# A set-attention and squared-ReLU kernel: the first batch planned anew, and second scores of the last batch made three groups at a time

## The chip, the cores and the metric

The kernel runs on one core of a Trainium2 chip. The metric is the device time of one execution in microseconds (us), the median of three runs. The engines are PE (matmul, with PEld for its weight loads), DVE, ACT, POOL and SP; SP issues all transfers here.

## The reference

`x` is (4, 12480, 128) in float32, `inducing` 32 points of 128. Two attentions follow each other, and an expert layer takes the result:

```python
def mab(q, kv):
    s = scale * (q @ kv.transpose(0, 2, 1))
    s = s - s.max(-1, keepdims=True)
    a = np.exp(s)
    a /= a.sum(-1, keepdims=True) + 1e-09
    return a @ kv
h = mab(I, x)            # the 32 points attend to all tokens of a batch
y = mab(x, h)            # every token attends to the 32 points
r = np.maximum(y @ w_in, 0.0)        # 128 -> 2048
out = (s * (r * r) + b) @ w_out      # 2048 -> 128
```

## The kernel before

**Tiles.** A batch has 12480 tokens: 26 blocks of 480 (`BLK`), 13 halves of two blocks, 7 groups of four blocks (`GR`); the last group, 6, has two. There are 104 blocks over four batches.

**The expert part** sets the pace. For a block and two of the 16 slices of 128 hidden units, `pair` (L917) makes two matmuls into an `h` buffer of PSUM (L928; three buffers, ring `h`), a relu `r` on ACT or DVE (L942, L944), a product with `h` on DVE (L965), a rounded square `g1` on ACT (L1010), and the rest `g2` on POOL or DVE (L987). `out_part` (L1024) multiplies these by `w_hi` and `w_lo`, the rounded and the remaining part of `w_out` times `s`: two matmuls of 480 columns in, six out (L1035). A block has eight pairs. The first eight pairs (`NATIVE`) take `w_out` unsplit in full float32, four passes each, and need no split halves. The weights of the first matmul, `wst`, are `w_in` times the attention's result, so that `y` itself is never made.

**The second attention** of a group is `attend` (L791): 8 score matmuls of 32 columns into the free one of two banks (`bank`), a transpose on DVE, maximum, subtraction, exponential on ACT, sum, reciprocal, product, transpose back, and a split into two halves `hl`, which SP spreads to tiles `a2t`. A block's output parts wait until the front work of the block before is done.

**The first attention** of the next batch runs beside it: `scores` (L681) per group, `top`, `values` (L717) per two groups, `sums`, `points`. A `visit` (L1073) lets PE make an attend's scores and up to two `side` units in a row, in one `h` buffer's halves; what it is made of says which block does what:

```python
ATTEND_AT = (2, 6, 10, 14, 18, 22)     # block of a batch at which group n + 1 is attended
SCORES_WITH, VALUES_WITH               # sides of these visits, per batch; VALUES_AT: alone
```

In the last batch there is no next one, so attends are alone.

**The opening** is batch 0's first attention, before any pair can start. `ORDER` (L66) is the order of SP's loads: `x` a group, `w_in` and `w_out` a chunk of 512 columns, `q` a group loaded already turned. For groups not in `TURNED`, PE turns each half with 8 transposes (`turn_x`, L444) and ACT copies it out. `p1_unit` makes a group's scores (L480), maximum on DVE (L484), exponentials (L493), their transposes (L500) and values (L511). The groups share four tiles, and turned copies share four others, so a load waits for the last use of its tile. Weights come as pairs of 32-bit words of float64 numbers and are made float32 by `narrow` (L324): three or four steps on DVE, two on ACT; `split_w_out` (L352) follows. After the last values come `h_sums`, `h_out` (hT, L620), `attend_first` (L837, block 0's attention weights by another way) and `w_first` (L624). Between these PE runs matmuls on zeros (`warm`, L1226).

**The order of work** comes from `Plan` (L95): every unit yields an engine, a planned duration and what it waits for, and the planner starts, per engine, the step with the least start time plus `WEIGHT` times urgency. Where a step may go to two engines, `LEAN` is added to their ends. The planned durations and urgencies are constants in the code; the result is a fixed order of instructions on each engine.

## Time and profile before

| what | us |
|---|---|
| median of three runs (lowest, highest) | 1551.55 (1551.47, 1551.56) |
| the profiled execution's own time | 1552.4 |
| its span, first to last instruction | 1550.6 |
| PE busy in the span | 1542.8 |
| DVE, ACT, POOL busy | 1469.9, 1482.0, 1471.1 |

Times in the profile are counted from the span's start. Busy time of PE is modelled for pipelined matmuls, so the distance from one matmul's start to the next tells more than the busy share. A mean granted clock of 1.00 is TensorE's higher level.

### The profile page before, as it was taken

The numbers are of one execution on the slowest core, as the hardware profiler recorded it, in microseconds if no ns is written. First come the engines' busy times: TensorE is split into PE (matmuls) and PEld (weight loads), VectorE is DVE, ScalarE is ACT, GpSimd is POOL, SyncE is SP. The second block draws the span as 40 slices with busy tenths as digits, with TensorE's granted clock in tenths as the row PEclk, the third lists the DMA queues.
The fourth block names the chain that finished last, engine by engine and source line by source line (L and its number), as shares of the span: only waits on it lengthen the run. The fifth ranks groups of instructions, "written<-read, shape, count | busy, mean of one in ns | idle before, by whom it ended". The sixth has DMA issues, their size and how long they took to land.

```text
span 1550.6 us, 24505 instructions
## 1 busy us (share of the span) xinstructions
PE 1542.8 (99%) x8135; PEld 1294.9 (84%) x8135; DVE 1469.9 (95%) x1648; ACT 1482.0 (96%) x1750; POOL 1471.1 (95%) x665
## 2 busy tenths in 40 slices
PE   9999999999999999999999999999999999999999
PEld 6688888888888888888888888888888888888887
DVE  5999999999999999999999999999999999999998
ACT  7899999999999999999999999999999999999998
POOL 0299999999999999999999999999999999999998
PEclk9999999999999999999999999999999999999999
DMA  8212321332233123123232321321313112112100
GB/s 300 64 56 80 122 72 71 114 130 96 68 111 115 39 103 115 39 103 115 71 85 80 118 76 66 115 80 65 112 60 96 32 52 71 40 44 71 57 22 32
DMA packets 53482, 130.12 MB, mean 84 GB/s; under 512 B 11262, under 2 KB 37758, under 8 KB 53358
## 3 DMA queue, kind: packets, MB, share of 16 engines
q1 hardware_dynamic: 53358, 128.56, 25.2%
q8 instruction: 66, 1.08, 0.3%
q14 instruction: 58, 0.48, 0.1%
HBM read 74.50 MB, written 25.56 MB: 65 GB/s over the span
## 4 chain that ended last, share of the span: by engine, by line
PE 96%; DMA 2%; DVE 1%; POOL 0%; issue 0%; ACT 0%; SPq 0%; ACTq 0%; DVEq 0%; POOLq 0%
PE x L1035 68%; PE h L928 23%; PE x L799 2%; PE h L742 1%; PE h L701 1%; DMA g<-in_w_in_dram 1%; DMA xn<-in_xQ_dram 1%; DMA s_sb<-in_s_rep_dram 0%; DVE g L965 0%; POOL g L987 0%; PE h L651 0%; ACT xn L214 0%; PE x L742 0%; PE x L511 0%; SPq L420 0%
## 5 line engine op out<-in xcount | busy, mean ns | idle before, releaser
L987 POOL TENSOR_TENSOR g<-g,g 128x960 fp32r<-128x960 f32 x657 | 1469.8, 2296 | 73.6 <-DVE g L965 67.8
L1035 PE MATMUL x<-g,w_hi 128*128 128x480 f32 x3296 | 1063.6, 375 | 0.0
L1010 ACT ACTIVATE g<-r 128x960 fp32r<-128x960 f32 (+1 forms) x805 | 796.2, 1029 | 16.5 <-DVE r L944 2.4
L965 DVE SCALAR_TENSOR_TENSOR g<-h,r 128x960 f32<-128x960 f32 x657 | 739.4, 1146 | 22.4 <-ACT r L942 14.2
L1035 PEld LDWEIGHTS x<-g,w_hi 128*128 128x128 f32 x3296 | 614.8, 187 | 91.8 <-POOL g L987 3.3
L942 ACT ACTIVATE r<-h 128x960 f32<-128x960 f32 x660 | 622.8, 969 | 27.3 <-PE h L928 26.3
L1035 PE MATMUL x<-g,w_lo 128*128 128x480 f32 x1648 | 617.3, 375 | 0.0
L928 PE MATMUL h<-a2t,wst 128*128 128x480 f32 x1664 | 484.7, 378 | 0.7 <-DVE g L965 0.7
L928 PEld LDWEIGHTS h<-a2t,wst 128*128 128x128 f32 x1664 | 306.6, 187 | 65.4 <-DVE x L805 7.3
L1035 PEld LDWEIGHTS x<-g,w_lo 128*128 128x128 f32 x1648 | 308.9, 187 | 42.8
L944 DVE TENSOR_SCALAR r<-h 128x960 f32<-128x960 f32 x172 | 197.7, 1150 | 9.5 <-PE h L928 7.1
L987 DVE TENSOR_TENSOR g<-h,g 128x960 fp32r<-128x960 f32 x167 | 192.6, 1154 | 12.7 <-ACT g L1010 1.3
L965 DVE SCALAR_TENSOR_TENSOR h<-h,r 128x960 f32<-128x960 f32 x167 | 193.1, 1157 | 6.4 <-ACT r L942 5.7
L1044 ACT ACTIVATE ob<-x,bias 128x480 f32<-128x480 f32 x103 | 68.0, 660 | 4.1 <-PE x L1035 3.9
L799 PE MATMUL x<-xt,hT 128*32 128x480 f32 x208 | 28.3, 578 | 0.0
L805 DVE STREAM_TRANSPOSE x<-x 128x480 f32<-128x480 f32 (+1 forms) x28 | 19.3, 688 | 2.2 <-PE x L799 2.1
L742 PEld LDWEIGHTS h<-xn,eT 128*32 128x32 f32 (+1 forms) x570 | 17.0, 109 | 5.0 <-issue 4.8
L823 DVE STREAM_TRANSPOSE x<-x 128x480 f32<-128x480 f32 (+1 forms) x28 | 19.5, 696 | 0.9
L742 PE MATMUL h<-xn,eT 128*32 128x128 f32 (+1 forms) x570 | 19.6, 273 | 0.0
L821 DVE TENSOR_TENSOR x<-x,l 128x480 f32<-128x480 f32 (+1 forms) x28 | 18.5, 661 | 0.7
L701 PE MATMUL h<-xt,ind_sb 128*32 128x480 f32 x156 | 19.1, 566 | 0.0
L810 DVE TENSOR_TENSOR x<-x,mx 128x480 f32<-128x480 f32 (+1 forms) x28 | 18.4, 656 | 0.1
(147 smaller groups left out, 375.4 us busy)
## 6 DMA issues: line engine op xcount, KB each, us to landing
xt<-in_xT_dram SPq DMA_DIRECT2D x41, 960.0 KB, 5.5
out_dram<-ob SPq DMA_DIRECT2D x104, 240.0 KB, 2.0
a2t<-hl SPq DMA_DIRECT2D x412, 60.0 KB, 2.0
xn<-in_xN_dram SPq DMA_DIRECT2D x18, 512.0 KB, 6.1
xn<-in_xN_dram SPq DMA_DIRECT2D x18, 448.0 KB, 6.7
r<-in_xH_dram SPq DMA_DIRECT2D x7, 480.0 KB, 8.2
xt<-in_xT_dram SPq DMA_DIRECT2D x7, 480.0 KB, 5.4
wst<-hl SPq DMA_DIRECT2D x48, 64.0 KB, 2.0
```

The costliest lines, as they stand in the source:

```text
L701: nc.tensor.matmul(ps[M * q:M * (q + 1), 0:BLK], ind_sb, xt[:, q], start=True, stop=True)
L742: nc.tensor.matmul(ps[M * c:M * (c + 1), 0:P], eT[0:rows, n], xn_tiles[b, g, half][0][0:rows, n - half * TH], start=m < P // M, stop=m + P ...
L799: nc.tensor.matmul(ps[M * q:M * (q + 1), 0:BLK], hT[:, 0:M], xt[:, q], start=True, stop=True)
L823: nc.vector.transpose(out=s, in_=s)
L928: nc.tensor.matmul(h[:, u, 0:BLK], wst[:, c * P:(c + 1) * P], A, start=True, stop=True)
L942: nc.scalar.activation(out=r, in_=hv, func=AF.Relu)
L944: nc.vector.tensor_scalar(out=r, in0=hv, scalar1=0.0, scalar2=None, op0=ALU.max)
L965: nc.vector.scalar_tensor_tensor(out=g, in0=hv, scalar=0.0, in1=r, op0=ALU.max, op1=ALU.mult)
L987: eng.tensor_tensor(out=g2, in0=g, in1=hi.bitcast(F32), op=ALU.subtract)
L1010: nc.scalar.activation(out=q["g1_t"][:, sl, :], in_=q["r_t"][:, sl, :], func=AF.Square)
L1035: nc.tensor.matmul(o, w, g, start=first and n == 0, stop=left == 0 and n == len(ops) - 1)
L1044: nc.scalar.activation(out=ob, in_=o, func=AF.Identity, bias=bias, scale=1.0 if scaled else s_sb)
```

## The change

**Opening.** `ORDER`, the homes of `x` (five tiles in place of four, `X_HOME`), and the planned durations are new; 54 single units get urgencies of their own (`URGENT`), and the planner adds 0.14 us when PE changes between tiled (32 columns) and whole matmuls. Group 6 is loaded turned as group 5 was; the turned loads have tiles of their own and wait for nothing. `x` 0's first half is loaded and turned in two parts. `s` and `b` are loaded last. `w_out`'s raw chunks get four tiles of their own, in which the split halves `w_hi` and `w_lo` are put later. In `narrow`, an ACT step may go to POOL; for three chunks (`POOLED`) a DVE step is made by ACT and POOL; the last product may go to POOL. The memset for the warming matmuls goes from POOL to DVE.

**Batch 0.** The scores of batch 1's groups 6, 4 and 5 (`GAP`) are made in the opening, once batch 0's values are done; their `x` is loaded there, and `attend(0, 0)` waits for two of them. The visits of batch 0 then have the sides that those of batches 1 and 2 have; values of groups 2 and 3 are no longer alone.

**Batch 3.** `LAST_WITH`: the scores of groups 2 and 3 are made in the visit of group 1, those of 5 and 6 in that of group 4. `turned_scores` transposes them into the SBUF tile `s`; `attend` of these groups then has no matmul and no first transpose, and its maximum and subtraction read that tile.

All other weights of the planner (`LEAN`, `R_LEAN`, `SLIP`, `OUT` and so on) have new values too.

```diff
--- before.py
+++ after.py
...
-LEAN = {'ACT': -0.5309, 'DVE': 0.6608}
-R_LEAN = {'DVE': -0.2301, 'ACT': -0.2128}
+LEAN = {'ACT': -1.8612, 'DVE': -0.9887}
+R_LEAN = {'DVE': -0.234, 'ACT': -0.174}
...
-TURNED = (5,)
-ORDER = (
-    ("x", 0), ("x", 1), ("w_out", 0), ("x", 2), ("w_out", 1), ("x", 3), ("w_in", 0), ("x", 4), ("w_in", 1),
-    ("w_in", 2), ("x", 5), ("x", 6), ("w_out", 2), ("q", 5), ("w_in", 3), ("w_out", 3),
-)
-WARM = 6
+TURNED = (5, 6)
+X_HOME = (4, 1, 3, 0, 3, 2, 1)
+GAP = (6, 4, 5)
+ORDER = (('x', 0), ('w_in', 1), ('x', 1), ('x', 2), ('w_out', 2), ('w_out', 1), ('w_in', 0), ('w_out', 3), ('x', 3), ('x', 4), ('x', 5), ('x', 6), ('n', 6), ('q', 5), ('w_in', 2), ('q', 6), ('w_in', 3), ('n', 4), ('n', 5), ('w_out', 0), ('s', 0))
+SWITCH = 0.14
+POOLED = (('w_in', 2), ('w_out', 0), ('w_out', 2))
+GAP_U = 107.5895
+WARM = 7
+URGENT = {
+    ('x', 3): -234.92,
+    ('w_in', 1): 384.17,
+    ('w', 1): 32.13,
+    ('n', 4): -165.82,
...
-SCORES_WITH = (((6,), (0, 1), (2, 3), (4, 5), (), ()), ((0, 1), (2, 3), (4, 5), (), (), ()), ((0, 1), (2, 3), (4, 5), (), (), ()))
+LAST_WITH = ((2, 3), (), (), (5, 6), (), ())
+SCORES_WITH = (((), (0, 1), (2, 3), (), (), ()), ((0, 1), (2, 3), (4, 5), (), (), ()), ((0, 1), (2, 3), (4, 5), (), (), ()))
-TOP_AT = (17, 11, 11)
-VALUES_WITH = (((), (), (), (), (0,), (2, 3)), ((), (), (), (0,), (1,), (2, 3)), ((), (), (), (0,), (1,), (2, 3)))
-VALUES_AT = (((1, 20),), (), ())
+TOP_AT = (11, 11, 11)
+VALUES_WITH = (((), (), (), (0,), (1,), (2, 3)), ((), (), (), (0,), (1,), (2, 3)), ((), (), (), (0,), (1,), (2, 3)))
+VALUES_AT = ((), (), ())
...
+                turn = SWITCH if u[9] is not None and u[9] != self.tiled else 0.0
+                able.setdefault(eng, []).append((at + turn + WEIGHT * urgency, at, engs[eng] + turn, u))
...
+    warm_sb = ew.tile([P, 512], F32R, name="g2", bufs=8)
+    nc.vector.memset(warm_sb.bitcast(F32), 0.0)
...
-    w_hi = const.tile([P, NF, P], F32R, name="w_hi")
-    w_lo = const.tile([P, NF, P], F32R, name="w_lo")
...
     def load_weight(gate, name, c):
-        turn, free = ring("g1", 4)
-        yield "SP", 0.45, free, *gate
...
-        raw = ew.tile([P, WC, 2], I32, name="g1", bufs=4)
+        if name == "w_in":
+            turn, free = ring("g1", 4)
+            yield "SP", 0.45, free, *gate
+            raw, used = ew.tile([P, WC, 2], I32, name="g1", bufs=4), ("g1", turn)
+        else:
+            yield "SP", 0.45, *gate
+            raw, used = w2_pool.tile([P, WC, 2], I32, name="w2"), ("raw used", c)
...
-        yield "ACT", 0.48
-        nc.scalar.activation(out=dst, in_=m, func=AF.Copy, scale=2.0**-20, bias=1.0)
+        yield dict(ACT=0.525, Pool=0.68), {"ACT": M_LEAN}, 0.0
+        if plan.eng == "ACT":
+            nc.scalar.activation(out=dst, in_=m, func=AF.Copy, scale=2.0**-20, bias=1.0)
+        else:
+            nc.gpsimd.tensor_scalar(out=dst, in0=m, scalar1=2.0**-20, scalar2=1.0, op0=ALU.mult, op1=ALU.add)
+        if name in POOLED:
+            yield "ACT", 0.525
+            nc.scalar.activation(out=m.bitcast(F32), in_=lo, func=AF.Copy, scale=2.0**-52)
+            yield "Pool", 1.37
+            nc.gpsimd.tensor_tensor(out=dst, in0=m.bitcast(F32), in1=dst, op=ALU.add)
+        else:
+            yield "DVE", 0.6, "both"
+            nc.vector.scalar_tensor_tensor(out=dst, in0=lo, scalar=2.0**-52, in1=dst, op0=ALU.mult, op1=ALU.add)
...
+        plan.set(used)
+        yield dict(DVE=0.6, Pool=1.37), 0.0, "both"
+        either().tensor_tensor(out=dst, in0=dst, in1=e.bitcast(F32), op=ALU.mult)
...
+    def split_weights(f, part):
...
+        at = w_order.index(f * P // WC)
+        return w2[at // 2][part][:, at % 2 * WC // P + f % (WC // P), :]
...
-        yield "ACT", 0.54, ("w_out", c)
-        nc.scalar.activation(out=w_hi[:, sl, :], in_=raw[:, sl, :], func=AF.Copy, scale=s_sb)
+        half = w_order.index(c) // 2
+        mine = w_order[2 * half:2 * half + 2]
+        yield "ACT", 0.615, "s", ("w_out", c), *[("raw used", n) for n in mine], ("w2", half - 1)
+        if half not in w2:
+            w2[half] = [w2_pool.tile([P, 2 * WC // P, P], F32R, name="w2") for _ in range(2)]
+        nc.scalar.activation(out=w_hi, in_=raw[:, sl, :], func=AF.Copy, scale=s_sb)
...
-            home["x", g] = g if g < 4 else 1 + (g - 4) % 3
+            home["x", g] = X_HOME[g]
...
+        for n, j in enumerate(turns):
+            home["xn", j] = xn[n % 4][0:T].rearrange("p n c -> p (n c)")
+        for n in range(SB):
+            home["xn", TURNED[0] * GR // SB + n] = turned_0[0:T, n * TH * P:(n + 1) * TH * P]
+        for g in TURNED[1:2]:
+            for n in range(SB):
+                t = p2.tile([P, 2, WC], F32, name="hl")
+                home["xn", g * GR // SB + n] = t[0:T].rearrange("p a t -> p (a t)")
...
-            yield "SP", 0.45, ("v done", j - 4)
-            nc.sync.dma_start(out=home["q"][j % 4], in_=xQ[j])
+            yield "SP", 0.45
+            nc.sync.dma_start(out=home["xn", j], in_=xQ[j])
...
-        yield "PE", 0.99, *waits, ("x half", j), ("v done", j - 4)
+        n = turns.index(j)
+        if j:
+            yield "PE", 0.88, "whole", *waits, ("x half", j), *([("v done", turns[n - 4])] if n > 3 else [])
+        else:
+            yield "PE", 0.44, "whole", *waits, ("x part", 0, 0)
...
+            if a and not j:
+                yield "PE", 0.44, "whole", ("x half", j)
...
-                "s": p1.tile([P, NG, BLK], F32, name="s"),
+                "s": st[0]["room"].rearrange("p (g t) -> p g t", g=NG) if b == 1 and GAP
+                else p1.tile([P, NG, BLK], F32, name="s"),
...
+    def turned_scores(b, g, ps, *waits):
+
+        rows = M * blocks_in(g)
+        yield "PE", 1.14, ("hT", b), ("x", b, g, 2), *waits
+        ps = ps()
+        scores_2(b, g, ps)
+        yield "DVE", 0.58
+        nc.vector.transpose(out=st[b]["s"][0:rows, g], in_=ps[0:rows, 0:BLK])
+        plan.set(("turned", b, g))
+
+    def attend(b, g, ps, *waits):
+        nb = blocks_in(g)
+        rows = M * nb
+        ahead = b == B - 1 and any(g in gs for gs in LAST_WITH)
+        if ahead:
+            yield "DVE", 0.57, ("turned", b, g), *waits
+            ps = ps()
+            s = ps[0:rows, 0:BLK]
+            v = s.rearrange("p (n i) -> p n i", i=M)
+            t = st[b]["s"][0:rows, g].rearrange("p (n i) -> p n i", i=M)
+        else:
+            yield "PE", 1.14, ("hT", b), ("x", b, g, 2), *waits
+            ps = ps()
+            scores_2(b, g, ps)
+            s = ps[0:rows, 0:BLK]
+            t = v = s.rearrange("p (n i) -> p n i", i=M)
...
-        yield "DVE", 0.58
-        nc.vector.transpose(out=s, in_=s)
-        yield "DVE", 0.57
-        mx = sm.tile([P, TB], F32, name="mx2")[0:rows]
-        nc.vector.reduce_max(out=mx, in_=v, axis=AX.X)
+        mx = ps[0:rows, BLK + TB:BLK + 2 * TB] if ahead else sm.tile([P, TB], F32, name="mx2")[0:rows]
+        nc.vector.reduce_max(out=mx, in_=t, axis=AX.X)
...
-        nc.vector.tensor_tensor(out=v, in0=v, in1=mx.unsqueeze(2).broadcast_to([rows, TB, M]), op=ALU.subtract)
+        nc.vector.tensor_tensor(out=v, in0=t, in1=mx.unsqueeze(2).broadcast_to([rows, TB, M]), op=ALU.subtract)
...
-                    yield (*want, ("ob", blk_g - 1) if blk_g else "first") if first else want
+                    start = [("ob", blk_g - 1)] if blk_g else ["first", *[("scores", 1, g) for g in GAP[0::2]]]
+                    yield (*want, *start) if first else want
...
-            side = []
+            side = [(turned_scores, b, g) for g in LAST_WITH[n]] if b == B - 1 else []
...
-                if n == 1:
-                    nc.sync.dma_start(out=s_sb, in_=s_rep)
-                    nc.sync.dma_start(out=b_sb, in_=b_rep)
-                plan.spawn(p1_work(n), FIRST + 0.1 * n)
+                plan.spawn(p1_work(n), FIRST + 0.1 * n + urgent("x", n))
                 for h in range(0 if n in TURNED else -(-blocks_in(n) // SB)):
-                    plan.spawn(turn_work(n, h), FIRST + 0.1 * n)
+                    plan.spawn(turn_work(n, h), FIRST + 0.1 * n + urgent("turn", n, h))
             elif what == "q":
                 yield from load_turned(n)
+            elif what == "s":
+                yield "SP", 0.9
+                nc.sync.dma_start(out=s_sb, in_=s_rep)
+                nc.sync.dma_start(out=b_sb, in_=b_rep)
+                plan.events["s"] = landing(1.0)
+            elif what == "n":
+                yield from load_xt((), 1, n, 1)
+                i = GAP.index(n)
+                plan.spawn(
+                    scores(1, n, (lambda: bank[1], lambda: hs[0][:, 0])[i % 2],
+                           ("p1", 0, NG - 1), *([("scores", 1, GAP[i - 2])] if i > 1 else [])),
+                    FIRST + GAP_U + i + urgent("n", n),
+                )
...
-    nc.gpsimd.memset(warm_sb.bitcast(F32), 0.0)
...
+        plan.set("warm done")
+
+    def h_free():
+        yield "SP", 0.0, "warm done", *[("scores", 1, g) for g in GAP[1::2]]
         plan.set(("h", 0))
...
-        plan.spawn(attend_first(lambda: bank[0]), FIRST)
+        plan.spawn(attend_first(lambda: bank[0]), FIRST + urgent("a"))
+        plan.spawn(h_free(), 0.0)
```

## Rows read from the trace of the kernel before

**Rows 1.** The page: busy time by engine, and shares of the last chain.
```profile
PE 1542.8 (99%) x8135; PEld 1294.9 (84%) x8135; DVE 1469.9 (95%) x1648; ACT 1482.0 (96%) x1750; POOL 1471.1 (95%) x665
...
PE 96%; DMA 2%; DVE 1%; POOL 0%; issue 0%; ACT 0%; SPq 0%; ACTq 0%; DVEq 0%; POOLq 0%
```

**Rows 2.** Windows, batches 0, 3: busy PE, PEld, DVE, ACT, POOL; clock, DMA, GB/s.
```profile
200.00:250.00 50.00, 50.00 (x239) 43.01 (x232) 48.24 (x52) 49.21 (x56) 50.00 (x23) 1.00 0.27 94
1350.00:1400.00 50.00, 50.00 (x238) 42.62 (x237) 49.05 (x51) 49.27 (x56) 50.00 (x24) 1.00 0.16 51
```

**Rows 3.** Timeline of PE in the opening: start, us, what, idle before.
```profile
4.40 1.93 PE L453 MATMUL h<-ident,xt 128*120 128x128 f32 x8
...
18.80 1.01 PE L480 MATMUL x<-r,ind_sb 128*32 128x480 f32 x8
...
20.77 1.08 PE L511 MATMUL x<-xn,eT 120*32 120x128 f32 x32
...
28.61 0.65 PE L500 MATMUL h<-ident,s 128*120 128x128 f32 x4
...
32.08 1.04 PE L453 MATMUL h<-ident,r 128*120 128x128 f32 x8
...
35.21 1.74 PE L511 MATMUL x<-xn,eT 120*32 120x128 f32 x44 [1.07 <-DMA xn<-in_xQ_dram]
...
46.36 1.06 PE L928 MATMUL h<-a2t,wst 128*128 128x480 f32 x4
```

**Rows 4.** Windows of the opening, as in rows 2.
```profile
0.00:10.00 10.00, 8.42 (x46) 5.55 (x46) 1.77 (x10) 3.91 (x6) 1.23 (x8) 1.00 0.70 221
10.00:28.00 18.00, 17.77 (x232) 11.63 (x232) 13.07 (x29) 16.39 (x33) 0.00 (x0) 1.00 1.01 406
35.00:45.00 10.00, 9.29 (x90) 6.60 (x91) 8.01 (x23) 5.61 (x12) 0.00 (x0) 1.00 0.10 41
```

**Rows 5.** Timeline of PE: a lone attend (batch 3), a visit (batch 0).
```profile
1214.65 0.59 PE L928 MATMUL h<-a2t,wst 128*128 128x480 f32 x2
1215.17 1.01 PE L799 MATMUL x<-xt,hT 128*32 128x480 f32 x8
1216.12 0.70 PE L1035 MATMUL x<-g,w_hi 128*128 128x480 f32 x2
1216.65 0.60 PE L928 MATMUL h<-a2t,wst 128*128 128x480 f32 x2
...
197.99 1.01 PE L799 MATMUL x<-xt,hT 128*32 128x480 f32 x8
200.54 0.70 PE L928 MATMUL h<-a2t,wst 128*128 128x480 f32 x2
```

**Rows 6.** Groups by shape: count, busy us, mean ns, idle before.
```profile
L987 POOL TENSOR_TENSOR g<-g,g 128x960 fp32r<-128x960 f32 x657 | 1469.8, 2296 | 73.6 <-DVE g L965 67.8 <-ACT g L1010 2.8 <-DVE x L821 1.2
...
L214 ACT COPY xn<-h 120x1024 f32<-120x1024 f32 x11 | 11.3, 1029 | 6.9 <-PE h L453 6.9
...
L810 DVE TENSOR_TENSOR x<-x,mx 128x480 f32<-128x480 f32 x24 | 15.8, 657 | 0.1
...
L348 DVE TENSOR_TENSOR w_in_sb<-w_in_sb,g 128x512 f32<-128x512 f32 x4 | 2.7, 682 | 0.0
...
L965 DVE SCALAR_TENSOR_TENSOR g<-h,r 128x960 f32<-128x960 f32 x657 | 739.4, 1146 | 22.4 <-ACT r L942 14.2
```

**Rows 7.** Chain that ended last, in the opening: start, us, what.
```profile
27.29 7.88 DMA xn<-in_xQ_dram
...
42.65 0.70 DVE wst L637
```

**Rows 8.** DMA issues: size of one, us to landing.
```profile
xt<-in_xH_dram SPq DMA_DIRECT2D x6, 480.0 KB, 6.4
...
g<-in_w_in_dram SPq DMA_DIRECT2D x4, 512.0 KB, 8.6
```

**Rows 9.** The same windows for the warming matmuls (L1231) alone.
```profile
38.00:46.40 8.40, 4.62 (x14) 2.47 (x14) 1.00 0.00 1
```

More of the change, by code (lines that the diff above doesn't have):

```diff
@@ L71 @@
 RUN = 512
+M_LEAN = 2.2035
 A_OFF = 19
@@ L121, in _step @@
             more = sum(w for w in waits if isinstance(w, float))
-            waits = [w for w in waits if not isinstance(w, float) and w != "both"]
-            self.units.append([unit, urgency + more, (ready, src), engs, waits, urgency, lean, None, both])
+            kind = True if "tiled" in waits else False if "whole" in waits else None
+            waits = [w for w in waits if not isinstance(w, float) and w not in ("both", "tiled", "whole")]
+            self.units.append([unit, urgency + more, (ready, src), engs, waits, urgency, lean, None, both, kind])
     def extend(self, us):
@@ L345, in narrow @@
         )
[L346 to L348 removed]
+        plan.set(used)
+        yield dict(DVE=0.6, Pool=1.37), 0.0, "both"
+        either().tensor_tensor(out=dst, in0=dst, in1=e.bitcast(F32), op=ALU.mult)
         plan.set(("g", e_turn))
         plan.set(name)
+    w2 = {}
+    w_order = [c for name, c in ORDER if name == "w_out"]
+    plan.events["w2", -1] = 0.0
+    def split_weights(f, part):
+        at = w_order.index(f * P // WC)
+        return w2[at // 2][part][:, at % 2 * WC // P + f % (WC // P), :]
     def split_w_out(c):
@@ L683, in scores @@
         rows = M * nb
-        if b not in st:
+        if b not in begun:
+            begun.add(b)
+            yield "DVE", 0.15, *waits
             d = st[b] = {
@@ L1034, in out_part @@
         for n, (w, g) in enumerate(ops):
-            nc.tensor.matmul(o, w, g, start=first and n == 0, stop=left == 0 and n == len(ops) - 1)
+            nc.tensor.matmul(o, w(), g, start=first and n == 0, stop=left == 0 and n == len(ops) - 1)
         used()
@@ L1051, in out_part @@
         plan.set(("ob", blk_g))
+    turned_0 = wst_pool.tile([P, F], F32, name="wst")
+    turns = [j for j in range(NSB) if j * SB // GR not in TURNED]
     w_out_raw = wst_pool.tile([P, NF, P], F32, name="wst")
@@ L1169, in tile_attn_relu2 @@
             for f, *args in (args[0], *args[1]) if f is visit else ((f, *args),):
-                if f in (scores, attend):
+                if f in (scores, turned_scores) or f is attend and not any(args[1] in gs for gs in LAST_WITH if args[0] == B - 1):
                     fetch(first + n - AHEAD, load_xt, *args, 1 if f is scores else 2)
```

243 lines of the change are left out of this document (152 added, 91 removed).

## The prediction

> **What bounds the kernel now.** I read three views in this order. First the page's busy shares and its chain: PE is busy 99% of the span and carries 96% of the chain that ended last, while DVE, ACT and POOL are each at 95 to 96% [rows 1]. A busy PE need not be PE at its peak, so I checked the spacing. The 50 us windows of batch 0 and of batch 3 both show PE at 50.00 [rows 2], and in the second 238 instructions, 8 of them the score matmuls of one attend. The other 230 are matmuls of 480 columns, which the planner spaces by 0.2134 us: 49.1 us, and the attend's 0.95 [rows 5] makes it 50. There is no slack on PE behind the opening. There, time falls only if PE gets less to do, and a plan with other weights can only lose.
>
> Second, the opening, where that does not hold: the first pair's matmul starts at 46.36 us, on a path of loads, ACT and DVE [rows 3]. Third, its windows: 221 GB/s of DMA in the first 10 us, then about 400 while loads are queued [rows 4]. The last output part and its store, which end the kernel, are not touched.
>
> **Term 1, PE work taken out behind the opening.** A lone attend costs PE more than its 8 score matmuls. Between the end of one pair of L928 (1214.65 + 0.427 = 1215.08) and the point from which the next matmuls are spaced normally (1216.65 − 0.427 = 1216.22) lie 1.14 us; from its first matmul to the next work it is 0.95 (1215.17 to 1216.12). A visit of an attend with two other groups takes 2.55 on that second count (197.99 to 200.54) [rows 5]. So two sides add 1.60, 0.80 each, and joining a visit instead of coming alone saves 1.14 − 0.80 = 0.34.
> - Scores of batch 1 for groups 6, 4 and 5 leave the visits of batch 0 for the opening: 3 × 0.80 = 2.40 us. Group 6 has half the blocks, but its matmuls run side by side, so I count it in full.
> - Values of groups 2 and 3, alone at block 20 before, join a visit: 0.34.
> - In the last batch groups 2, 3, 5 and 6 are scored inside two visits: 4 × 0.34 = 1.36.
>
> Sum 4.1 us, all on the path, since PE is the path. Against it: the four moved groups hold a half of an h buffer until DVE has transposed them into SBUF. The first batches do the same with two sides, and PE stays at 50.00 there [rows 2], so I count nothing; without that cover PE would lose a DVE operation of this size per moved group, 4 × 0.66 [rows 6] = 2.6 us at most. DVE's own work is unchanged in number: the transpose moves to the visit, and maximum and subtraction read SBUF instead of PSUM. The trace has no such form; the subtraction in PSUM [rows 6] is the nearest and stands for it, a tenth less or more. DVE has 2% left in batch 3 [rows 2], and saving 1.4 us of 370 asks 0.4% of it.
>
> **Term 2, the opening.** Up to the last value matmuls (35.21 + 1.74 = 36.95) PE works 32.6 us from 4.40 on, and waits 1.07 us for the turned copy of group 5 [rows 3]. SP issued that load only when an earlier buffer was free, and the path hangs on the transfer for 7.88 us [rows 7]. The change gives turned loads homes of their own, so that wait goes, and loads group 6 turned as well, so 8 transposes (1.04 us [rows 3]) and one ACT copy (1.03 us [rows 6]) go. PE alone would be done 2.1 us earlier, at 34.8.
>
> Is the DMA in time? Up to q5 there are 10.5 MB in the new order, up to q6 11.5 (a half of x 0.49, a weight chunk 0.52 [rows 8]). With 2.2 MB moved by 10 us and 0.41 MB per us from then on [rows 4], q5 is in at 10 + 8.3/0.41 = 30.2 and q6 at 32.7. The last x has five weights ahead of it, as before, and comes at 26.6. Late next is x3: three weights more stand ahead of it, 6.55 MB, in at 20.6, where its scores run at 18.80 now. PE then has left two full groups, each 2 × 1.04 of transposes, 1.01 of scores, 0.65 and 1.08 for exponentials and values [rows 3], 4.8 us; 2.7 for group 5, which has no transposes, and 1.9 for the smaller group 6: 14.2 us, and 34.8 again. So the gain up to here is 2.1. On SP's queue n6 waits for x3 and n4 for x6, with n5, w_out 0 and s behind; the DMA has a backlog until about 34 us, which covers these waits.
>
> From there to the first pair is a chain of 9.4 us through hT and attend_first [rows 3]. Two weight subtractions on DVE stand inside it; the first, 0.70 us at 42.65 [rows 7], delays it in whole, the second I count with 0.3. The new urgencies put the chain ahead of them: 1.0 us less. Term 2 is 3.1; I take 3.0.
>
> Against it: the three early scores put 2.4 us on PE, hidden by the 4.6 us of warming matmuls [rows 9], and 3 × 0.66 us on DVE [rows 6], which idles 2.0 us of the 10 from 35 to 45 [rows 4]; cost 0 to 2.0, taken as 0 because weight work leaves DVE for POOL. And w_out chunk 0 lands at about 40, last but for s. Its seven steps of narrowing, 0.4 to 0.7 us each after the row of L348 [rows 6], take five or six us with hand-overs: 46 to 50. Native pairs 0 and 1 need it, and pair 3 takes the g buffer after it. Until then PE has six pairs' first matmuls, the attend and pair 2's output, 2.6 + 1.1 + 1.6 = 5.3 us from 43.3. Cost 0 to 2, taken as 0: it is nearer to being covered. Better packing than I assume could bring the DMA's limit (33.1) instead of PE's, 1.7 more.
>
> Edits with no price of their own: the warm-up memset goes from POOL to DVE, both idle until x0 is in at 4.40; s and b are loaded last, for splits that wait for chunk 0 anyway; the split halves live where raw chunks were, read out by 50 and needed by pair 8 after eight native pairs.
>
> **Sum.** 4.1 + 3.0 = 7.1 us off the profiled execution's 1552.4 (span 1550.6): 1545.3. The median of the runs shown, 1551.55, is 0.85 below that execution, so 1544.5. A difference under 0.2%, 3.1 us, is about what this measurement cannot tell from none.
>
> **Rivals.**
> - **The opening gives nothing.** POOL waits 67.8 us now, nearly all before its first such operation [rows 6], and does nothing in the opening's windows [rows 4]; the change gives it additions of three weight chunks and offers it products of all. On 512 columns I estimate 2.30 × 512/960 = 1.2 us each, from the only POOL operation of that kind in the trace [rows 6]. If DVE is held back while one runs, six to eight of them take 7 to 10 us of DVE, far more than it has free, and 3 or more come to lie on the way to the first pair. For it: the 0.68 us of L348 was taken with POOL idle. Against: POOL is busy all the time later and DVE still does L965 in 1.15 [rows 6], about what its other operations on 960 columns take. Time 1551.55 − 4.1 = 1547.5; with 1.5 us lost, 1549. The Trainium skill (SBUF — State Buffer, the engine side) has the rule: a DVE operation with two SBUF inputs and a GpSimd operation take a shared port pair in turn, the later one blocked for the whole instruction. L965 reads h from PSUM and L348 has two SBUF inputs, so by that rule the price would be paid; no row before shows it. Chance 0.24.
> - **The opening gives more**, down to the DMA's limit and a quicker chain behind it: 4.1 + 6.4 off, 1541. Chance 0.16.
> - **DVE or ACT becomes the bound, and it is slower.** All the planner's weights move, the leans that split copies and squares between ACT and DVE among them. With DVE and ACT at 98% in batch 3 [rows 2], a wrong choice leaves PE short for a moment. Place: every block. Price: 103 blocks × 0.1 us = 10.3; with 7.1 gained, 1554.7. It decides from 0.07 us per block. For it, engines near 98%; against, a PE without gaps under the old weights. Chance 0.07.
> - **The change does not do what it says**: merged visits stall the pairs by what they save, and early scores meet their waits; 2.7 and at most 1 remain, 1548. Chance 0.05.
>
> **How the numbers follow.** Forecast 0.48: 1544.5, its own range 1542 to 1547.3. The range runs from 1540.5 (the larger opening gain) to 1549 (none, and 1.5 given back) and leaves out the slower case and the tails. Faster by over 3.1 us (under 1548.4): forecast, larger gain and two thirds of the first rival, 0.80. Within: 0.13. Slower: 0.07.
>
> **What would show it.** Right: the first L928 at about 43.3 instead of 46.36; the last value matmuls done by 35; two runs of L799 for three groups in batch 3, and PE at 50.00 in every window behind the opening. Wrong: waits of PE in those windows; the successor of L348 at over 0.7 us beside POOL; a granted clock under 1.00 in the opening; a first pair later than 45.

## The result and the profile after

The changed kernel takes 1567.36 us (median of four runs, 1567.02 to 1569.32) beside 1551.55 for the kernel before: ratio 1.0103 [1.009, 1.0116], 15.8 us slower, where 7 us less were forecast. The profiled execution is the longest of the four, 1569.3 (span 1567.5). Its page, and from the page of before the two groups that the prediction did not show:

```profile
PE 1551.4 (99%) x8123; PEld 1303.7 (83%) x8123; DVE 1480.5 (94%) x1656; ACT 1470.2 (94%) x1724; POOL 1475.9 (94%) x675
...
L1188 PE MATMUL x<-g,w 128*128 128x480 f32 x4944 | 1190.9, 377 | 0.9 <-DVE hl L983 0.5
```

```profile
L1035 PE MATMUL x<-g,w_hi 128*128 128x480 f32 x3296 | 1063.6, 375 | 0.0
L1035 PE MATMUL x<-g,w_lo 128*128 128x480 f32 x1648 | 617.3, 375 | 0.0
```

PE is busy 8.6 us longer than before [rows 1], though it has less to do, and one of its 4944 output matmuls takes 2 ns more, 377 for 375. Such a duration is longer than the distance between two matmuls, since they overlap, so I took the distance from each start to the next from the trace (pairs nearer than 240 ns, behind 100 us): 213.4 ns before, 215.6 after. 4944 x 2.2 ns is 10.9 us, spread over the whole kernel. It is not waiting: behind 60 us PE's waits come to 1.3 us after and 0.7 before (what PE waited for: us in total, times, longest):

```profile
PE x L1188 <- DVE hl L983: 0.5, 1, 0.5
PE x L1188 <- POOL g L1140: 0.4, 1, 0.4
PE h L1081 <- DVE g L1118: 0.4, 1, 0.4
```

```profile
PE h L928 <- DVE g L965: 0.7, 2, 0.4
```

Windows (columns as in [rows 2]) show PE full in batch 3 as before. Their counts of instructions do not compare: all 235 are whole matmuls here, while 8 of the 238 before are the scores of a lone attend. The other three rows are the opening's:

```profile
30.00:35.00 5.00, 4.06 (x39) 2.70 (x37) 3.62 (x9) 4.92 (x11) 0.00 (x0) 1.00 1.01 226
35.00:40.00 5.00, 2.18 (x64) 1.64 (x56) 0.53 (x3) 0.00 (x1) 0.00 (x0) 1.00 1.05 241
40.00:45.00 5.00, 3.48 (x33) 3.02 (x34) 2.87 (x9) 2.94 (x8) 2.50 (x3) 0.66 0.98 382
...
1350.00:1400.00 50.00, 50.00 (x235) 43.60 (x233) 47.44 (x46) 48.34 (x57) 49.17 (x23) 1.00 0.26 90
```

From 30 to 40 us the DMA engines are busy all the time and move 226 to 241 GB/s, not about 400 [rows 4]; DVE (0.53 us) and ACT all but stand still from 35 to 40, PE works 2.2 us of 5, and behind that pause its granted clock falls to 0.66 on the mean of five microseconds. The chain of waits names the transfer, the turned copy of group 6, and what it delays:

```profile
29.76 12.01 DMA hl<-in_xQ_dram
...
55.71 1.74 DVE w L460
57.45 0.03 issue
57.48 0.68 DVE s L834 x2
58.16 0.04 issue
58.20 1.01 PE x L927 x8
```

Timeline of PE:

```profile
41.91 1.71 PE L634 MATMUL x<-hl,eT 120*32 120x128 f32 x14 [0.78 <-DMA hl<-in_xQ_dram]
...
52.31 0.69 PE L1081 MATMUL h<-a2t,wst 128*128 128x480 f32 x2 [0.15 <-ACT a2t L279]
...
58.20 1.01 PE L927 MATMUL x<-r,hT 128*32 128x480 f32 x8 [1.18 <-DVE s L834]
...
60.53 1.80 PE L1188 MATMUL x<-g,wst 128*128 128x480 f32 x4
```

The first pair's matmul comes at 52.31, not 46.36 [rows 3], and the first output part at 60.53 instead of 49.75. A first pair later than 45 us and a granted clock under 1.00 were two of the prediction's signs of being wrong. ACT starts to copy block 0 out of PSUM at 77.9 us, 66.9 before. The profile of `e1_addr`, with the same list of work, has it at 75.3: this opening varies by some 2 us between executions, and the profiled one is a late one.

So there were two losses to explain: some 9 to 11 us in the opening, and about 11 spread behind it.

### The profile page after: what moved, and what is told of

Read it like the earlier page. It is cut to its first block, busy times and chain, and to the rows that moved or that the text cites. A ratio compares the mean times of both kernels' runs of the same rounds, so it can differ in the third digit from the quotient of the medians.

```text
span 1567.5 us, 24472 instructions
## 1 busy us (share of the span) xinstructions
PE 1551.4 (99%) x8123; PEld 1303.7 (83%) x8123; DVE 1480.5 (94%) x1656; ACT 1470.2 (94%) x1724; POOL 1475.9 (94%) x675
## 4 chain that ended last, share of the span: by engine, by line
PE 96%; DMA 1%; DVE 1%; ACT 1%; issue 0%; SPq 0%; POOL 0%; DVEq 0%; ACTq 0%; POOLq 0%
PE x L1188 68%; PE h L1081 23%; PE x L927 1%; PE h L872 1%; PE h L831 1%; DMA hl<-in_xQ_dram 1%; PE h L574 0%; DMA r<-in_xH_dram 0%; DVE g L1118 0%; ACT g L1163 0%; PE x L634 0%; ACT r L1095 0%; PE x L602 0%; PE h L927 0%; PE h L776 0%
## 5 line engine op out<-in xcount | busy, mean ns | idle before, releaser
L1188 PE MATMUL x<-g,w 128*128 128x480 f32 x4944 | 1190.9, 377 | 0.9 <-DVE hl L983 0.5
L1188 PEld LDWEIGHTS x<-g,w 128*128 128x128 f32 x4944 | 927.8, 188 | 137.9 <-DVE hl L983 1.2
L1095 ACT ACTIVATE r<-h 128x960 f32<-128x960 f32 x652 | 614.1, 968 | 46.9 <-PE h L1081 43.9
L1081 PEld LDWEIGHTS h<-a2t,wst 128*128 128x128 f32 x1664 | 310.0, 188 | 62.3 <-issue 6.5
L1097 DVE TENSOR_SCALAR r<-h 128x960 f32<-128x960 f32 x180 | 206.6, 1149 | 13.0 <-PE h L1081 11.3
L1140 DVE TENSOR_TENSOR g<-h,g 128x960 fp32r<-128x960 f32 x168 | 193.5, 1152 | 10.8 <-ACT g L1163 0.7
L927 PE MATMUL x<-xt,hT 128*32 128x480 f32 x172 | 23.3, 578 | 0.0
L967 DVE TENSOR_REDUCE x<-x 128x15 f32<-128x480 f32 (+1 forms) x28 | 18.3, 655 | 0.7 <-ACT x L965 0.7
L983 DVE TENSOR_TENSOR hl<-x,hl 128x480 fp32r<-128x480 f32 (+1 forms) x28 | 17.9, 640 | 0.0
```

What stands on the lines that cost most here:

```text
L927: nc.tensor.matmul(ps[M * q:M * (q + 1), 0:BLK], hT[:, 0:M], xt[:, q], start=True, stop=True)
L1081: nc.tensor.matmul(h[:, u, 0:BLK], wst[:, c * P:(c + 1) * P], A, start=True, stop=True)
L1095: nc.scalar.activation(out=r, in_=hv, func=AF.Relu)
L1097: nc.vector.tensor_scalar(out=r, in0=hv, scalar1=0.0, scalar2=None, op0=ALU.max)
L1140: eng.tensor_tensor(out=g2, in0=g, in1=hi.bitcast(F32), op=ALU.subtract)
L1188: nc.tensor.matmul(o, w(), g, start=first and n == 0, stop=left == 0 and n == len(ops) - 1)
```

## Experiments

Medians, with the ratio to the kernel before, measured beside each, and its 95% interval:

| run | us | ratio |
|---|---|---|
| e1_addr | 1556.52 | 1.0029 [1.0016, 1.0041] |
| e2_pad | 1562.37 | 1.0072 [1.0057, 1.0087] |
| e3_both | 1552.49 | 1.0008 [0.9998, 1.0017] |
| e4_before_addr | 1562.23 | 1.0070 [1.0055, 1.0085] |
| e5_no_gap | 1560.29 | 1.0055 [1.0040, 1.0071] |
| e6_no_last | 1552.70 | 1.0010 [1.0001, 1.0018] |
| e7_x1_first | 1569.97 | 1.0122 [1.0108, 1.0136] |
| e8_no_pooled | 1565.12 | 1.0090 [1.0076, 1.0103] |
| e9_defer | 1552.88 | 1.0009 [0.9999, 1.0019] |
| e10_gap_out | 1552.00 | 1.0002 [0.9992, 1.0011] |
| e11_shift32 | 1562.56 | 1.0070 [1.0055, 1.0085] |
| e12_before_pad | 1550.91 | 0.9996 [0.9986, 1.0005] |
| e13_g_off | 1575.21 | 1.0143 [1.0128, 1.0158] |
| e14_plus1024 | 1551.94 | 0.9999 [0.9989, 1.0008] |
| e15_no_lock | 1551.74 | 0.9998 [0.9989, 1.0008] |
| e17_three_out | 1551.80 | 0.9996 [0.9987, 1.0006] |
| e18_w_in2_out | 1550.98 | 0.9997 [0.9988, 1.0007] |
| e19_before_g_off | 1561.48 | 1.0061 [1.0044, 1.0078] |

### The place of the weights, and the copies of 120 rows

The built programs give each tile's address. `w_hi` and `w_lo` began at bytes 9024 and 17216 of a partition; the new `w2` tiles begin at 10240, 14336, 18432 and 22528, because five small constants now lie in front of them. The columns that they are multiplied with (`g1`, `g2`) did not move.

`e1_addr`, on the changed kernel:

```diff
+    const2 = ctx.enter_context(tc.tile_pool(name="const2", bufs=1))   # behind w2_pool
-    bias = const.tile([P, 1], F32, name="bias")
+    bias = const2.tile([P, 1], F32, name="bias")
...
```

> Only the place of the split weights in SBUF changes: five small constants come behind the four w2 tiles, which then begin at byte 9024 of a partition (in the kernel before the two weight tiles were at 9024 and 17216; in the changed one the four tiles are at 10240 to 22528, all multiples of 512). Every engine's order of instructions is that of the changed kernel. Theory A (place): the out matmuls' spacing falls from 215.6 ns on average to the 213.4 of before, 4944 x 2.2 ns = about 11 us less, so 1556, with the opening as late as in the changed kernel (first output part at 60.5 us). Rival B (the new plan: ACT, DVE and POOL now collide with PE's reads in another way): no change, 1567.

`e4_before_addr`, the mirror of it, on the kernel before:

```diff
-    w_hi = const.tile([P, NF, P], F32R, name="w_hi")
-    w_lo = const.tile([P, NF, P], F32R, name="w_lo")
...
     sel = const.tile([P, P], F32, name="sel")
+    w_hi = const.tile([P, NF, P], F32R, name="w_hi")
+    w_lo = const.tile([P, NF, P], F32R, name="w_lo")
```

> The kernel before, with w_hi and w_lo made after the five small constants, so that they lie at bytes 10240 and 18432, the addresses that the changed kernel uses; nothing else. Theory A: the out matmuls' spacing rises from 213.4 ns to about 215.6, and the time from 1551.55 to about 1562. Rival B: no change, 1551.5.

Measured: 1567.36 becomes 1556.52 (10.8 less) in the one, and 1551.34 (the kernel before, measured beside it) becomes 1562.23 (10.9 more) in the other. The groups of `e1_addr` and of `e4_before_addr`:

```profile
L1189 PE MATMUL x<-g,w 128*128 128x480 f32 x4944 | 1181.5, 375 | 1.3 <-POOL g L1141 0.7
```

```profile
L1035 PE MATMUL x<-g,w_hi 128*128 128x480 f32 x3296 | 1072.6, 378 | 0.0
L1035 PE MATMUL x<-g,w_lo 128*128 128x480 f32 x1648 | 619.9, 376 | 0.0
```

Spacing: 213.4 ns in `e1_addr`; in `e4_before_addr` 216.6 on `w_hi`, 214.0 on `w_lo`. Not an instruction of the plan differs, so the whole spread loss is the place of the weights, shown in both directions.

`e2_pad` gives the copies all 128 rows (`e3_both` has this and `e1_addr`'s edit):

```diff
-            x[0].reshape(...).reshape(-1, T, SB * NQ * C)
+            np.pad(x[0].reshape(...).reshape(-1, T, SB * NQ * C), ((0, 0), (0, P - T), (0, 0)))
...
-                    xn[n // SB][:, n % SB, q, :], start=(q == 0), ...
+                    xn[n // SB][0:T, n % SB, q, :], start=(q == 0), ...
```

> The turned copies xQ get 8 rows of zeros, so each load writes all 128 partitions instead of 120; same plan, 7% more bytes in these three loads. Theory C (loads of 120 rows run slow): the DMA moves about 400 GB/s from 29 to 37 us instead of 225 to 240, the copy of group 6 lands at about 34 to 36 instead of 41.8, PE's wait for it and the half-clock stretch go, and the opening is 5 to 8 us shorter: about 1560 to 1562. Rival D (too much is queued; whatever loads in that stretch is slow, or two copies and the weights get into each other's way): still about 230 GB/s, landing at about 42, and the time 1567.

> Both edits: weights at byte 9024 and copies with 128 rows. If A and C both hold and add: 1567.4 - 11 - 5 to 8 = 1548 to 1551, a little below the kernel before. If only A holds 1556, if only C 1560 to 1562, if neither 1567.

1562.37: 5.0 less, at the lower end of what was expected. Windows of `e2_pad`:

```profile
30.00:35.00 5.00, 3.86 (x81) 3.13 (x79) 3.52 (x11) 3.71 (x9) 0.56 (x1) 1.00 1.03 422
35.00:40.00 5.00, 5.00 (x57) 3.95 (x56) 3.05 (x12) 2.03 (x6) 2.22 (x3) 1.00 0.86 339
```

422 GB/s where there were 226, PE full from 35 to 40, and the clock stays at 1.00. 7% more bytes arrive much sooner. Transfers of 120 rows are what is slow, and not the number of loads. The traces' records of single packets show the form of it: from 30 to 35 us a packet of 4096 bytes takes 287 ns on the median in the changed kernel, 273 in the kernel before, and 159 in `e2_pad`, which is also what one takes from 10 to 15 us in all three. The Trainium skill (DMA: Bandwidth & Descriptors, "Why a DMA increments its semaphore by 16 and not by 1") says that a transfer is split over the largest number of engines up to 16 that divides its rows: 15 for 120 rows. One engine in sixteen less would be 6%, an estimate from that rule; the traces do not tell the number of engines, and they show 226 for 422 by slower packets, so the rule does not give the size. What in the chip makes the packets slow, no run shows.

Both edits together: 1552.49, 14.9 of the 15.8 us back. Why it is not the 1544.5 of the forecast stays open up to here. The same padding on the kernel before:

```diff
-        home["q"] = [t[0:T].rearrange("p n c -> p (n c)") for t in xn]
+        home["q"] = [t.rearrange("p n c -> p (n c)") for t in xn]
```

> The kernel before with xQ of 128 rows, nothing else. Theory C (the copies of 120 rows are slow in any order): from 28 to 35 us about 400 GB/s instead of 221 to 246, the copy of group 5 lands 2 to 3 us earlier, PE's wait of 1.07 us for it goes, and the time falls by 1 to 2 us: 1549.5 to 1550.5. Rival D (only two copies in flight beside the change's other loads are slow): no change, 1551.5.

The landings of the two copies take 5.0 us on the median instead of 6.6, PE's wait of 1.07 [rows 3] is gone, and every block of the profiled execution is 1.3 us earlier. The time, 1550.91, is 0.9 below the kernel before, measured beside it at 1551.77; the interval still holds 1, so a gain in the time is likely but not shown. It is the one version here that does the whole computation with a median below both kernels.

### Which property of the place

`e11_shift32` puts 32 bytes in front of the weights of `e4_before_addr`; `e14_plus1024` puts `ident` and `sel`, 1024 bytes, in front of those of before; the other two change `G_OFF`, from which word of a `g1` or `g2` half the columns begin:

```diff
-G_OFF = 3
+G_OFF = 19
```

> The kernel before with its weights behind the small constants, as in the run that put them at 10240 and 18432 (1562.2), and 32 bytes more in front of them: 10272 and 18464. Theory (what costs is that the rows of the weights begin at a multiple of 512 bytes): spacing 213.4 ns and 1551.5 again. Rival (it is the neighbourhood of the address, or the place of the constants in front): 215.6 and 1562.

> The kernel before with ident and sel, 1024 bytes, put in front of the weights, so that these begin at 10048 and 18240: 1024 further than before, 192 less than in the slow arrangement (10240, 1562.2). Theory H: modulo 128, 256, 512 and 1024 they stand as before to the moving columns: 213.4 ns and 1551.5. Rival (the neighbourhood from about 10000 bytes on is what is slow): 215.6 ns, 1562.

> The changed kernel with one constant changed: the 480 columns of every g1 and g2 half begin 19 words into their 512 instead of 3, 64 bytes further; weights stay at 10240 to 22528. Nothing else. Theory H (what counts is where the weights lie against the moving columns, within some power of two of bytes; before, the columns began 12 bytes behind the weights' place modulo 128, and after the change 76 behind): 12 behind again, spacing 213.4 ns, 1567.4 - 11 = 1556. Rival (the absolute place of the weights counts, or a finer or wider relation): 215.6 ns and 1567.

> The kernel before with G_OFF 19 in place of 3: the columns of g1 and g2 begin 64 bytes further, the weights stay at 9024. Counted as the columns' first byte less the weights' first byte modulo 512, the arrangements so far are: 140 (before, and moved by 1024): 213.4 ns; 460 (changed kernel) and 428 (moved by 32): 215.6 to 216.5 on the w_hi matmuls; 12 (changed kernel with G_OFF 19): 217.0. Here it is 204, which modulo 256 is that of the slow 460. If the relation counts modulo 256 or less: slow, 215 to 217 ns and about 1562. If modulo 512 or more, with 140 and 204 in its good part: 213.4 ns and 1551.5.

The groups of `e13_g_off`, of `e14_plus1024` and of `e19_before_g_off`:

```profile
L1188 PE MATMUL x<-g,w 128*128 128x480 f32 x4944 | 1197.8, 379 | 0.4 <-DVE hl L983 0.4
```

```profile
L1035 PE MATMUL x<-g,w_hi 128*128 128x480 f32 x3296 | 1063.4, 375 | 0.0
```

```profile
L1035 PE MATMUL x<-g,w_hi 128*128 128x480 f32 x3296 | 1069.1, 377 | 0.0
L1035 PE MATMUL x<-g,w_lo 128*128 128x480 f32 x1648 | 621.7, 377 | 0.0
```

A start of the weights at a multiple of 512 bytes is not it (`e11_shift32`: 1562.56, spacing 216.4 on `w_hi`), nor the neighbourhood of the address (`e14_plus1024`: 1551.94, 213.4). Moving the columns alone makes the good kernel slow (`e19_before_g_off`: 1561.48) and the slow one slower (`e13_g_off`: 1575.21, spacing 217.0). So the place of the columns counts as well as that of the weights.

In `e11_shift32` the built program has the columns 32 bytes further too, as all tiles behind the weights. Weights and columns thus moved together, their distance stayed at 460 (the 428 for this run in the last text above is wrong), and the spacing stayed that of `e4_before_addr` (216.4 on `w_hi` and 214.1 on `w_lo`, beside 216.6 and 214.0). First byte of the columns less first byte of the weights, modulo 256, is 140 in the three arrangements at 213.4 ns; it is 204 in the changed kernel, `e4_before_addr`, `e11_shift32` and `e19_before_g_off`, and 12 in `e13_g_off`, all slow. Modulo 128, the 12 of the slow `e13_g_off` would equal the 12 of the good ones, so theory H fails in that form, and modulo 256 is the smallest power of two that separates them.

This points to where weights and columns lie against each other, but does not prove it. In all three good arrangements the weights begin at 64 modulo 256 and the columns at 204, so each could also have a good place of its own; the run that would decide, both moved together out of a good arrangement, was not made. Nor does the distance modulo 256 say everything: `e19_before_g_off` has 215.4 ns on `w_hi` and 216.0 on `w_lo`, another division than `e4_before_addr` at the same 204. How the good range is bounded, and what in the chip does it, no run shows.

### What the opening still loses

In `e3_both` block 0 leaves PSUM at 70.6 us, 3.75 later than before, where the prediction had 3.0 earlier. The first pair is not late there: its matmul comes at 45.03, 1.3 us earlier than before. The first output part comes at 53.24, 3.5 later. From the one to the other are 8.2 us, 3.4 before (46.36 [rows 3] to 49.75). PE in `e3_both`, and the first output part of the kernel before:

```profile
45.03 0.70 PE L1082 MATMUL h<-a2t,wst 128*128 128x480 f32 x2
...
53.24 1.80 PE L1189 MATMUL x<-g,wst 128*128 128x480 f32 x4
```

```profile
49.75 1.77 PE L1035 MATMUL x<-g,wst 128*128 128x480 f32 x4
```

Four edits of `e3_both` went through the planner anew, the last of batch 3 (`e6_no_last`, further down):

```diff
-GAP = (6, 4, 5)                       # e5_no_gap; sides of batch 0's visits as in the kernel before
+GAP = ()
-LAST_WITH = ((2, 3), (), (), (5, 6), (), ())       # e6_no_last
+LAST_WITH = ((), (), (), (), (), ())
-('x', 0), ('w_in', 1), ('x', 1),      # e7_x1_first
+('x', 0), ('x', 1), ('w_in', 1),
-POOLED = (('w_in', 2), ('w_out', 0), ('w_out', 2))  # e8_no_pooled
+POOLED = ()
```

> On the version with weights at byte 9024 and copies of 128 rows (1552.5): the scores of batch 1's groups 6, 4 and 5 go back from the opening to the visits of batch 0, as in the kernel before; everything else stays as changed. Theory E (the early scores are not hidden: three DVE operations of 0.73 us each and both banks of x stand ahead of block 0's attend and first output parts): first output part at 50 to 51 us instead of 53.2, so 2.5 to 3 us less in the opening, and 2.7 us more in blocks 1 to 22: 1552 to 1553 in all, with block 0 about 3 us earlier. Rival F (they lie beside other work, as the prediction had it; it is the late weights that hold the first pairs): block 0 as late as with them, and 1555.

> On the same version: x 1 is loaded ahead of w_in 1, which was second. In the changed order DVE's first operation on w_in 1 stands in its queue ahead of the identity's conversion and of the first maximum, and waits for that chunk until 8.2 us, while the scores were done before. Theory G (the early weight costs the first attention its predicted gain of 2 us): first maximum at about 7.4 us instead of 9.2, last values done at about 35 instead of 36.8, and 1550.5 to 1551.5. Rival: the first attention is bound by the loads behind, last values at 36.8, 1552.5.

> On the same version: the three weight chunks whose sum POOL made are summed on DVE again (one operation of 0.69 us on DVE in place of one of 1.3 on POOL and one of ACT). In the version's profile the split of the last w_out chunk took DVE 1.73 us while POOL's sum ran, 0.74 in the kernel before. Theory (DVE is held while POOL adds): that split takes 0.74 again in this run, and the time stays within 1 us of 1552.5, since DVE gets the sums back. Rival (the 1.73 us has another cause, such as the tiles): it stays at 1.7.

The three that concern the opening are far slower than any theory had it (1560.3, 1570.0, 1565.1) and tell little of what they were made for: the planner wrote another list from the first microseconds on, and the list got worse in places that the edit does not touch. In `e7_x1_first` block 0 is 7 us later than before, and blocks 20 to 77 lose another 6; PE waits there:

```profile
PE x L1189 <- ACT g L1164: 2.9, 4, 1.5
PE h L1082 <- DVE g L1119: 1.9, 5, 0.5
```

All waits of PE behind 60 us come to 0.7 us in the kernel before. One thing `e8_no_pooled` does show: the split of `w_out` on DVE takes 0.71 us (1.42 for two) with no sum on POOL beside it.

The next edits therefore left the planner's list as it is and changed only what is issued. `e9_defer` issues DVE's first operation on `w_in` 1 one place later. `e10_gap_out` replaces the early scores' DVE operation:

```diff
-        nc.vector.tensor_scalar(out=d["s"][0:rows, g], in0=ps[0:rows, 0:BLK], ..., accum_out=...)
+        if b == 1 and g in GAP:
+            nc.gpsimd.memset(d["s"][0:rows, g], 0.0)
...
-            nc.gpsimd.tensor_tensor(out=dst, in0=m.bitcast(F32), in1=dst, op=ALU.add)      # e15_no_lock
+            if name != ("w_out", 0):
+                nc.gpsimd.tensor_tensor(out=dst, in0=m.bitcast(F32), in1=dst, op=ALU.add)
```

> On the version with both edits (1552.5), without a new plan: the planner's list stays word for word, but DVE's first operation on w_in 1 is issued together with its second, one place behind the first maximum. Nothing is left out. Theory G (this operation, waiting for its load at the head of DVE's queue, delays the first attention): first maximum at 7.9 us instead of 9.2, what follows on PE up to 1.3 us earlier, block 0 and the end 0.5 to 1.3 us earlier: 1551.2 to 1552. Rival (PE waits for the loads of x behind it anyway): 1552.5. The order of all engines' later work is unchanged, so nothing else can differ.

> On the same version, same list: the three early scores lose their DVE operation (the copy with maximum out of PSUM); POOL writes zeros there instead, so the second batch's attention leaves out the scores of groups 4, 5 and 6. PE still makes their matmuls. Theory E (these operations stand ahead of attend_first's and block 0's chain): x's second attention starts 1.5 to 2.2 us earlier than 50.9, first output part at 51 to 51.7 instead of 53.2, the end 1.5 to 2.2 us earlier: 1550.3 to 1551. Rival F (DVE has other work to wait for there, the late weights): less than 0.5 us.

> On the version with both edits, same list: POOL's sum for w_out chunk 0 is left out, so that chunk keeps only the high words of its numbers. Theory (DVE's split of w_out was held for 1.0 us by this sum, and block 0's attend waits behind it): the split takes 0.74 us instead of 1.73, x's second attention starts at about 49.9 instead of 50.9, block 0 is 1.0 us earlier, the end 1.0 earlier: 1551.5. Rival (something else is late next, such as the third early score's maximum or the weights): under 0.4 us.

`e9_defer` gains nothing (1552.88): the first maximum stays at 9.17, released by PE's scores, not by DVE's queue. Theory G falls. `e10_gap_out` gains 0.5 us (block 0 1.1 earlier), `e15_no_lock` 0.75 (block 0 0.6 earlier). Gains of this size are at the edge of what can be told: the intervals above reach 1.5 us to either side, and block 0 comes between 70.0 and 70.6 us in the four profiles with this opening unchanged (`e2_pad`, `e3_both`, `e6_no_last`, `e9_defer`), as it does in `e15_no_lock`. The split on DVE in `e3_both`, POOL's operation beside it, and the split in `e15_no_lock`:

```profile
48.43 1.73 DVE L461 SCALAR_TENSOR_TENSOR w<-wst,s_sb,w 128x512 fp32r<-128x512 f32 x1
...
48.33 1.29 POOL L425 TENSOR_TENSOR wst<-g,wst 128x512 f32<-128x512 f32 x1 [1.41 <-ACT g L423]
```

```profile
48.77 0.75 DVE L462 SCALAR_TENSOR_TENSOR w<-wst,s_sb,w 128x512 fp32r<-128x512 f32 x1
```

DVE starts 0.1 us behind POOL and ends 0.5 us behind POOL's end; without POOL's operation it takes 0.75. The Trainium skill (SBUF — State Buffer, "SBUF: two separate sides") says that a DVE operation with two inputs in SBUF and a GpSimd operation that reads SBUF lock one port pair against each other; this trace agrees, at a price of 1.0 us for this operation.

`e17_three_out` leaves out both of these and the last two steps of `w_in` 3, `e18_w_in2_out` both and the same steps of `w_in` 2:

> On the same version, same list: three things are left out together: the DVE operations of the early scores (POOL writes zeros instead), POOL's sum for w_out 0, and the last two steps of narrowing w_in chunk 3 (0.68 and 0.69 us on DVE; PE's matmul for that chunk's weights waits for the second until 45.9 us). If the three stand one behind the other on DVE, their gains add: about 1.1 (measured) + 1.0 + 1.4 = 3.5 us, block 0's eviction at 67.4, as in the kernel before, and 1549. If one covers another, or PE's first attention is what is late, clearly less.

> The run before (all but two early scores' DVE work out, no POOL sum for w_out 0) left out the wrong weight's steps: its trace shows that those of w_in 3 stood at 40.8 us, and that the two at 44.3 and 45.2, which release PE's matmul at 45.9, are chunk 2's. So now, on the version with both edits and the same list: the early scores' DVE operations, POOL's sum for w_out 0, and the last two steps of chunk 2 of w_in (not 3) are left out. Theory F (this weight is what PE's last weight matmuls wait for): they start at about 44.6 instead of 45.95, and block 0's eviction comes at about 68.4 instead of 69.7, the end 1.3 us earlier, 1550.4. Rival (PE's own work there, 3 early scores and the weights' matmuls, is late next): under 0.5 us earlier.

`e17_three_out` gains 0.7 us, not 3.5; its trace shows that the steps I had taken for chunk 3's belong to chunk 2, as the text of the run after it says. `e18_w_in2_out` brings 1550.98, 0.8 less again (block 0 at 68.9, 1.8 us earlier than in `e3_both`). PE in `e17_three_out` and in `e18_w_in2_out`:

```profile
45.95 2.19 PE L761 MATMUL h<-w_in_sb,hT 128*128 128x512 f32 x4 [0.20 <-DVE w_in_sb L439]
```

```profile
38.96 0.96 PE L1004 MATMUL x<-hT,r 128*120 128x32 f32 x8
39.84 1.01 PE L835 MATMUL h<-xt,ind_sb 128*32 128x480 f32 x8
...
42.70 1.00 PE L835 MATMUL x<-xt,ind_sb 128*32 128x480 f32 x4
...
45.34 1.88 PE L761 MATMUL h<-w_in_sb,hT 128*128 128x512 f32 x4
47.15 1.01 PE L835 MATMUL x<-xt,ind_sb 128*32 128x480 f32 x8
...
51.49 1.77 PE L1196 MATMUL x<-g,wst 128*128 128x480 f32 x4
```

With DVE's three charges gone PE hardly waits from the scores of `attend_first` (38.96) to the first output part at 51.49, and still this stretch is 12.5 us long, 10.0 before (39.73 to 49.75). The early scores (L835) take three times about a microsecond of it. That their PE time is on the path there is read from this trace; no run took it out alone.

### Batch 3

> On the same version: batch 3's attends alone again, nothing else changed; the order of work is the same up to that batch. The prediction's term: 4 x 0.34 = 1.36 us, so 1553.85. Rival: the blocks of batch 3 gained only about 0.5 us against those of batch 2 in the changed kernel, so about 1553.0, because the moved groups cost the pairs something else.

1552.70 beside 1552.49: the merged visits are worth 0.2 us, within what the runs scatter. PE in `e3_both`, a visit of three groups:

```profile
1214.26 1.01 PE L928 MATMUL x<-xt,hT 128*32 128x480 f32 x8
1215.09 1.79 PE L928 MATMUL h<-xt,hT 128*32 128x480 f32 x16
...
1504.76 0.70 PE L1082 MATMUL h<-a2t,wst 128*128 128x480 f32 x2
1506.26 0.69 PE L1189 MATMUL x<-g,w 128*128 128x480 f32 x2 [0.80 <-POOL g L1141]
```

Summed over the batch, the time between expert matmuls around attends is 6.2 us with lone attends (1.03 each, the short group too) and 5.3 with two visits of 2.64: 0.9 saved. One new wait of 0.80 for POOL, at 1506 us, takes most of it back; `e6_no_last` has waits of 0.2 in this batch.

## Why the prediction was wrong

**Failed, the largest: an edit priced at nothing.** "The split halves live where raw chunks were, read out by 50 and needed by pair 8" looked at when the tiles are free, not at where they lie. The 49.1 us for 230 matmuls at 0.2134 were taken to hold for the changed kernel. Their new place costs 2.2 ns per output matmul, 10.8 us (`e1_addr`, `e4_before_addr`); no rival had it.

**Failed: the arrival of q5 and q6 at 0.41 MB/us.** The trace of before had the warning in one of its rows: the path hung 7.88 us on the second of two copies of 120 rows [rows 7], while weights and x of 128 rows came at 406 GB/s [rows 4]. I put that wait down to the buffer that SP waited for. The window from 30 to 35 us of before, 237 GB/s at a DMA share of 0.96, would have told:

```profile
30.00:35.00 5.00, 3.86 (x57) 2.87 (x55) 3.82 (x12) 4.65 (x12) 0.00 (x0) 1.00 0.96 237
```

In the changed kernel, where a third such copy was added, q6 landed at 41.8 us, not at 32.7. Price: 5.0 us (`e2_pad`).

**Failed: "the gain up to here is 2.1", the first attention.** With the copies mended the last values are done at 36.8, not 34.8. PE is not the only path there: in `e3_both` it waits 1.5 us for ACT's exponentials, 0.9 for ACT's copy and 0.8 for x 1, which stands behind `w_in` 1 now. `e9_defer` excludes DVE's queue; no run without a new plan separates ACT from the load, so that part is open.

**Failed: the early scores "hidden by the 4.6 us of warming matmuls", and "cost 0 to 2.0, taken as 0".** With copies and weights mended, the first output part comes 8.2 us behind the first pair in place of 3.4, and the prediction had taken both of its costs there as 0. The early scores cost 0.5 us on DVE (`e10_gap_out`), up to 2 to 3 on PE by the trace of `e18_w_in2_out`, which no run took out alone. `w_out` chunk 0 was rightly a worry, by another way: not its own lateness, but POOL's sum for it, which holds DVE (0.75, `e15_no_lock`); and chunk 2 of `w_in`, which the text did not name, is narrowed late (0.8, `e18_w_in2_out` against `e17_three_out`).

**Right: the chain to the first pair 1.0 us shorter.** In `e3_both` it takes 8.2 us from the last values (36.81 to 45.03), where before it took 9.4. It did not help: the first output part still comes 3.5 us later than before.

**Right: term 1 in batch 0.** 3 x 0.80 + 0.34 = 2.74. Against the kernel before, `e3_both` is 3.2 us late in blocks 0 to 3 and 0.7 in blocks 20 to 25, 2.5 gained, and between 75 and 480 us the time between expert matmuls falls from 23.8 to 21.2 us.

**Too large: term 1 in batch 3**, 1.36: 0.9 on PE, 0.2 in the time.

**The rivals.** POOL's hold of DVE (0.24) exists, but is worth about 0.75 us and not the whole opening. A time behind 1551.55 was given 0.07, for ACT and DVE falling short in every block; the slower result came by another mechanism, and that one was seen only in the versions planned anew. "A plan with other weights can only lose" is borne out: three of the four new plans lost 8 to 17 us.

The sum, at medians: 1567.4 less 1544.5 is 22.9 us; 10.8 place of the weights, 4.0 more for the copies on top of that, 1.5 for DVE's three charges (`e18_w_in2_out`), 1.2 in batch 3. Some 5 us stay without a run of their own. By the trace of `e3_both`, 2 of them lie in the first attention (36.8, not 34.8); the rest lies between the first pair and the first output part, where the early scores on PE are the candidate. That is argued from traces, not shown.

## What to carry to other kernels

When a change moves a tile that TensorE reads in a stream of matmuls, compare the spacing of starts before and after, even where no instruction is new: here the same instructions took 1% longer, and the order of five small constants decided it. Give a transfer all 128 rows, with padding if need be, and suspect the transfer itself where the DMA is busy and moves half of what it moved a moment ago. A list from a planner is one point of a rough landscape: test a part of a change in the list as it is, since three of four new plans cost 8 to 17 us here, one of them from a single moved load.
